# Second-weight sums on two engines, and preparation ahead of feed-forward items, in a fused attention and feed-forward kernel

## The chip, the cores and the metric

One core of a Trainium2 chip runs the whole program. The metric is the device time of one execution in microseconds (us); a comparison uses the median of several runs. The engines are TensorE (PE in the profile; PEld is its loading of weights), VectorE (DVE), ScalarE (ACT) and GpSimd (POOL); SyncE (SP) issues the transfers. Each engine works through its own queue in the order in which the program emitted its instructions, and waits on semaphores for the others.

## The reference

Two blocks follow each other. The first is routed attention over 4 batches, 8 heads, 768 positions and 64 values a head: every query and key is assigned to one of 16 clusters, and a query attends only to keys of its own cluster.

```python
q_assign = argmax(einsum('bhsd,hcd->bhsc', q_n, c_n))      # and k_assign
mask = q_assign[:, :, :, None] == k_assign[:, :, None, :]
attn = softmax(where(mask, scale * q @ k.T, -1e9))
x = (attn @ v) laid out as (3072 tokens, 512)
```

The second is a feed-forward block with 2048 hidden values: `h = x @ w_in`, `g = h * clip(h + 3, 0, 6) / 6`, `out = g @ w_out`. The weights arrive as 64-bit floats and are turned into 32-bit ones on the chip ("decoding").

## The kernel before

**Attention.** Two heads form a pair; there are 16 pairs of 12 steps each, 192 steps in all, and 48 steps make a batch. The main loop takes two steps at a time (n is the first of them, r its place in its pair). A step's scores are made by `scores` (PE, tile ps), turned into exponentials by `exponentials` (ACT, tile ex, line 463), and added up over keys by `key_sums` (POOL, tile acc, lines 484 and 487). `attn_v` multiplies ex with the values (PE, tile pv) and copies the result (ACT, num). After six steps `sum_up` adds acc over partitions (PE, tile pd, line 521), and `inverse` takes the reciprocal of pd on DVE (rcp, line 527) and multiplies num with it; a transfer keeps num in memory.

**Preparation of the next pair.** While a pair runs, the next one is prepared: `turn` transposes q and k on PE (pqk, line 318), ACT copies them (xf, line 324); `cluster_scores` makes pcs (line 335), copied by ACT to cs; `route` transposes it (pr), and DVE finds the maximum and the one-hot rows (lines 349, 355); `route_turn` transposes those (po, line 379), and ACT copies them to xm (line 384). Before step 96 (DECODED) the tiles pqk, pcs, pr, po, pd and the feed-forward's ph all take turns on two PSUM buffers (pool psum_m, tag m). From step 96 on, pqk, pcs, pr, po and pd share one PSUM buffer (pool psum_t), so that a pcs behind a pd waits for the reciprocal of that pd.

**Feed-forward.** A block is 256 tokens; the 12 blocks are worked off as "items" that the main loop takes from a list, fill, as steps allow. The first block's eight `up` items (PE, tile ph, line 643, then `lift` on ACT, `clip` on DVE and `gated_sums` on POOL, line 678) run singly at steps 60, 64, 70, 74, 80, 84, 90 and 94, and its seven `down` items (X and Y, line 723) after step 96. Products are in a form with seven multiplications instead of eight for each 2x2 split, so sums of weights are needed: `weight_sums` makes T1 to T4 of the second weights (line 577, two halves each, eight instructions on DVE; T3 overwrites a part of w_out_sb), and `make_first_sums` makes those of the first weights (line 610, four DVE instructions of 128x256 for each of eight i, called in the first block's down items: two in item 0, one in each later item). Down item 0 and 1 read T2, item 2 T1, item 3 T3, item 6 T4.

**The order.** It is written by hand: instructions are emitted in the order of the loop and no scheduler moves them. Within one pass of the loop before step 96: scores, exponentials, key sums, attn_v, the division if six steps are complete; then feed-forward items and preparation, one of each in turn, item first; then a number of decoding steps given by `share`. The list of decoding steps ends with the eight weight sums; share gives 6, 5, 4, 3, 5, 5 of them at r = 0, 2, 4, 6, 8, 10. So weight sums 0 to 2 fall at step 90 and 3 to 7 at step 92, and the division of step 92 (pd, rcp) stands among them on DVE.

Of the kernel before, what the change touches and what calls it, by code (L numbers as in the profile page):

```python
# [12 lines left out]
ALU = mybir.AluOpType  # L13
# [103 lines left out]
def fast_path(ctx, tc, ok, q, k, v, centroids, moe_w_in, moe_w_out, out):  # L117
# [3 lines left out]
    nc = tc.nc  # L121
    PSUM = bass.MemoryType.PSUM

    def pool(name, bufs, **kw):
        return ctx.enter_context(tc.tile_pool(name=name, bufs=bufs, **kw))
# [44 lines left out]
    st = {}  # L170
# [11 lines left out]
    def load(g, *names):  # L182
        if g >= NPAIR:
            return
        b, h = divmod(2 * g, H)
        for name in names:
            if name == "v":
                dst = st["v", g] = vp.tile([P, 2, NCH, D], F32, name="vt")
            elif name == "q":
                st["qk", g] = qkp.tile([P, 2, NCH, 2, D], F32, name="qk")  # L190
            if name != "v":
                dst = st["qk", g][:, "qk".index(name)]
            src = {"q": q, "k": k, "v": v}[name]
            for t in range(2):
                nc.sync.dma_start((dst[:, t] if name == "v" else dst[:, :, t]), src[b, h + t].rearrange("(p j) d -> p j d", p=P))
# [9 lines left out]
    def load_weights(i):  # L205
        if i < len(chunks):
            st["raw", i] = rawp.tile([P, WC, 2], U32, name="raw")
            nc.sync.dma_start(st["raw", i], chunks[i][1])
# [56 lines left out]
    def constants():  # L265
        make_identity(nc, ident)
        for t in range(2):
            nc.vector.tensor_reduce(
                out=parity[:, t : t + 1],
                in_=ident.rearrange("p (h t c) -> p t h c", t=2, c=C)[:, t], axis=AX.XY, op=ALU.max,  # L270
            )
        nc.gpsimd.memset(half_c, 0.5)
        nc.gpsimd.memset(low_c, 1.0 / BOUND)
        nc.gpsimd.memset(ones, 1.0)
        nc.gpsimd.memset(w_low, W_LOW)
        nc.gpsimd.memset(one_hot, 0.0)
        for c in range(C):
            nc.gpsimd.memset(number[:, 0, c : c + 1], c - C * (C - 1) / 2.0)
            nc.gpsimd.memset(number[:, 1, c : c + 1], -float(c))

        st["warm"] = psum_t.tile([P, 4, P], F32, name="warm", tag="t")
        idle(14)
# [5 lines left out]
    def centroid_norm():  # L288
        cn = unit_rows(nc, startp, cen, D)

        nc.scalar.activation(out=w_totals[:, 0, 0:1], in_=w_low, func=ACT.Exp)

        wide = startp.tile([P, 2, D], F32, name="cenwide")
        for t in range(2):
            nc.vector.tensor_scalar_mul(out=wide[:, t], in0=cn, scalar1=parity[:, t : t + 1])
        st["wide"] = wide
# [10 lines left out]
    def turn(g, part):  # L307
        if part == 0:
            st["xf", g] = xp.tile([P, NC2, P], F32, name="xf")
        qk, xf = st["qk", g], st["xf", g]  # L310
        pt = scratch([P, 4, P], "pqk")
        for i in range(4):
            j = part * 4 + i
            if g == 0 and j == NCH:

                idle(5)
                centroid_turn()
            nc.tensor.transpose(out=pt[:, i], in_=qk[:, j // NCH, j % NCH], identity=ident)  # L318
        dst = xf[:, part * 4 : part * 4 + 4]

        if g == 0 and part == 2:
            nc.vector.tensor_copy(out=dst, in_=pt)
        else:
            nc.scalar.copy(out=dst, in_=pt)
        if part == 2:
            st.pop(("qk", g))
# [4 lines left out]
    def cluster_scores(g):  # L331
        c0, xf = (2 * g) % H * C, st["xf", g]
        ps = scratch([P, 512], "pcs")[:, 0 : NC2 // 4 * P]
        for a in range(4):
            nc.tensor.matmul(  # L335
                ps[a * 2 * C : (a + 1) * 2 * C], lhsT=cnT[:, c0 : c0 + 2 * C], rhs=xf[:, a::4],
                start=True, stop=True,
            )
        cs = st["cs", g] = rtp.tile([P, NC2 // 4, P], F32, name="cs")
        nc.scalar.copy(out=cs, in_=ps)  # L340
# [168 lines left out]
    def divide(n):  # L509
        return sum_up(n)()  # L510
# [52 lines left out]
    wb = [[w_out_sb[:, t * HF : (t + 1) * HF, c * HC : (c + 1) * HC] for c in range(2)] for t in range(2)]  # L563

    def weight_sums(i):
        if i == 0:
            decoding.close()
            wtp = pool("wtp", 1)
            for name in ("T1", "T2", "T4"):
                st[name] = wtp.tile([P, HF, HC], F32, name=name)  # L570
            st["T3"] = wb[0][1]
        name, a, b = (
            ("T1", wb[0][1], wb[0][0]), ("T2", wb[1][1], st["T1"]), ("T4", wb[1][0], st.get("T2")),
            ("T3", wb[1][1], wb[0][1]),
        )[i // 2]
        h = slice(i % 2 * HF // 2, (i % 2 + 1) * HF // 2)
        nc.vector.tensor_tensor(out=st[name][:, h], in0=a[:, h], in1=b[:, h], op=ALU.subtract)  # L577

# [256 lines left out]
    per_pair = 2 * NCH  # L837
# [11 lines left out]
    READY, DECODED = per_batch + 2 * lag_d, 2 * per_batch  # L849

    def share(n, r):

        if n < READY:
            return {0: 4, 2: 3, 4: 3, 6: 1, 8: 2, 10: 4}[r]
        return {0: 6, 2: 5, 4: 4, 6: 3, 8: 5, 10: 5}[r]

    def items_by(n):

# [60 lines left out]
    with tc.manual_schedule():  # L919
        nc.scalar.dma_start(cen, centroids.rearrange("h c d -> (h c) d"))  # L920
        load(0, "q", "k")
        constants()
        load(0, "v")
        load_weights(0)
        centroid_norm()
        for part in range(3):
            turn(0, part)
        nc.vector.tensor_copy(out=ident_q, in_=ident)
        load(1, "q", "k")
        load_weights(1)  # L930
        cluster_scores(0)
        scores_qk(0)
        route(0)
        scores_qk(1)
        for part in range(2):
            route_turn(0, part)

        for n in range(0, total + lag_d + 2, 2):
            g, r = divmod(n, per_pair)
            fours = n >= DECODED  # L940
            steps = [i for i in (n, n + 1) if i < total]
            prep = prep_items(g + 1, r, fours)
            if fours:
                four_by_four(n, r, steps)
            else:
                for i in steps:
                    scores(i)
                    exponentials(i)
                    key_sums(i)
                for i in (n - lag_v, n - lag_v + 1):  # L950
                    if i >= 0:
                        attn_v(i)
                m = n - lag_d + 1
                if m >= 0 and m % NCH == NCH - 1:
                    later.append(divide(m))
                    ready(m)
            if prep and r == (6 if fours else 4):
                prep.pop(0)()
            if n == DECODED:
                st["early"] = False  # L960
            if r == 6 and not fours:
                load(g + 2, "q", "k")
                load(g + 1, "v")
            if not fours or r % 4 == 2 or n >= total:
                want = min(items_by(n + 2) - st["done"], len(fill))
                st["done"] += want
                for i in range(max(len(prep), want)):
                    if i < want:
                        fill.pop(0)()
                    if i < len(prep):  # L970
                        prep[i]()


                    for _ in range({6: 2 * (i > 0), 10: 2 * (i > 0)}.get(r, 2)):
                        if singles:
                            singles.pop(0)()
                if fours:
                    for op in singles + numbers:
                        op()
                    singles.clear(), numbers.clear()  # L980
            if r == 6 and fours:
                load(g + 2, "q", "k")
                load(g + 1, "v")
            for step in decode[: share(n, r)]:
                step()
            del decode[: share(n, r)]
            if not fours:
                for op in numbers:
                    op()
                numbers.clear()  # L990
                check_all()
            checks.extend(later)
            later.clear()

        while checks:
            check_all()
            checks.extend(later)
            later.clear()
        st["last"] = True
        flag = whether_good()  # L1000
        while fill:
            fill.pop(0)()
            if len(fill) == HOLD // 2:
                flag()
# [363 lines left out]
```

## Time and profile before

| what | value |
|---|---|
| median of 3 runs | 1006.48 us (1006.28 to 1008.38) |
| span of the profiled execution | 1007.6 us |
| PE busy | 987.3 us, 98% |
| DVE busy | 659.3 us, 65% |
| ACT, POOL busy | 389.5 us (39%), 431.7 us (43%) |
| PE idle in 125 to 150, 150 to 200, 200 to 225, 225 to 250 us | 2.05, 1.63, 2.02, 1.90 us |
| weight sums (line 577) | eight, 232.0 to 248.9 us, 1.22 us each at the shortest, 2.83 at the longest |
| steps 60 to 94 (first ph to last ph) | 138.0 to 240.9 us |

A row of a timeline gives the start, the duration, the engine, the line and operation, what is written from what, the shape, the count of equal instructions that follow each other, and in square brackets how long the engine had been idle and what it then waited for. A row with a count has the duration of all of them together. Windows give a stretch, its width, the busy time of each engine in it with the number of instructions, the granted clock of PE, the share of the transfer engines and GB/s.

### The profile page before, as it was taken

How to read it: one execution, taken by the hardware profiler on the slowest of the kernel's cores; microseconds unless marked ns; L12 is line 12 of the kernel's file. 1: busy time of each engine (PE TensorE's matmuls, PEld its weight loads, DVE VectorE, ACT ScalarE, POOL GpSimd, SP SyncE). 2: the span in 40 equal slices, each digit the busy share in tenths (PEclk: the TensorE clock that was granted, in tenths of full speed). 3: DMA queues.
4: the chain of work that ended last, by engine and by line, in shares of the span. 5: the costliest groups of instructions: out<-in, count | busy, mean ns of one | idle time of the engine just before them, and what ended most of it. 6: DMA issues, size and time to landing. Idle time of an engine off the chain costs nothing.

```text
span 1007.6 us, 16709 instructions
## 1 busy us (share of the span) xinstructions
PE 987.3 (98%) x6421; PEld 731.7 (73%) x6421; DVE 659.3 (65%) x1255; ACT 389.5 (39%) x762; POOL 431.7 (43%) x379
## 2 busy tenths in 40 slices
PE   8999999999999999999999999999999999999997
PEld 5444445545788777778787777777777898999996
DVE  6789988989856158376667577558657372727270
ACT  5888877684234134233333333333223020202020
POOL 3877766765425335335425335426336030303030
PEclk9999999999999999999999999999999999999999
DMA  7345554531253043123323224123123141414120
GB/s 188 94 126 147 143 171 131 154 83 53 98 165 100 14 128 92 39 69 104 85 83 95 56 82 109 37 71 101 36 79 92 34 142 36 132 40 129 48 69 25
DMA packets 91018, 92.70 MB, mean 92 GB/s; under 512 B 54321, under 2 KB 74801, under 8 KB 90929
## 3 DMA queue, kind: packets, MB, share of 16 engines
q1 hardware_dynamic: 90208, 90.98, 31.8%
q8 instruction: 53, 0.87, 0.4%
q10 hardware_dynamic: 720, 0.56, 0.2%
q14 instruction: 37, 0.29, 0.1%
HBM read 75.79 MB, written 15.73 MB: 91 GB/s over the span
## 4 chain that ended last, share of the span: by engine, by line
PE 73%; DVE 5%; ACT 1%; issue 1%; ACTq 0%; DVEq 0%
PE Y L723 17%; PE uY L688 14%; PE X L723 12%; PE uX L688 11%; PE ps L436 8%; PE pv L497 7%; PE pqk L318 1%; PE pd L521 1%; DVE sx L699 1%; PE ph L643 1%; DVE g_sb L699 1%; PE pcs L335 1%; DVE g_sb L556 1%; DVE ps L472 1%; DVE T L577 1%
## 5 line engine op out<-in xcount | busy, mean ns | idle before, releaser
L487 POOL TENSOR_TENSOR acc<-acc,ex 128x768 f32<-128x768 f32 x128 | 243.5, 1902 | 161.7 <-ACT ex L463 155.9
L678 POOL TENSOR_TENSOR g_sb<-g_sb 128x256 f32<-128x256 f32 x176 | 126.3, 739 | 281.3 <-DVE g_sb L556 269.7
L463 ACT ACTIVATE ex<-ps 128x768 f32<-128x768 f32 x192 | 147.4, 805 | 83.2 <-PE ps L436 64.0
L553 ACT ACTIVATE sx<-g_sb,half_c 128x512 f32<-128x512 f32 x88 | 63.5, 722 | 264.9 <-DVE g_sb L699 254.2
L436 PE MATMUL ps<-xf 64*128 64x384 f32 x768 | 157.0, 499 | 1.3 <-ACT ex L463 0.6
L497 PE MATMUL pv<-ex,vt 128*64 128x384 f32 x768 | 142.4, 499 | 0.4 <-ACT num L503 0.4
L497 PEld LDWEIGHTS pv<-ex,vt 128*64 128x64 f32 x768 | 48.4, 137 | 85.1 <-issue 74.9
L484 POOL TENSOR_TENSOR acc<-ex 128x768 f32<-128x768 f32 x32 | 59.1, 1846 | 103.3 <-ACT ex L463 103.2
L730 DVE TENSOR_TENSOR y<-y,Y 128x256 f32<-128x256 f32 x48 | 20.2, 421 | 125.5 <-PE Y L723 124.7
L472 DVE TENSOR_SCALAR ps<-xm,kid 128x384 f32<-128x384 bf16 x144 | 83.7, 616 | 26.4 <-ACT ex L463 23.2
L527 DVE RECIPROCAL rcp<-pd 128x384 f32<-128x384 f32 x32 | 81.7, 2554 | 24.4 <-PE pd L521 23.7
L436 PEld LDWEIGHTS ps<-xf 64*128 64x128 f32 x768 | 66.6, 188 | 40.6 <-issue 22.3
L688 PE MATMUL uX<-xb,w_in_sb 128*128 128x128 f32 x704 | 93.0, 275 | 0.0
L723 PE MATMUL X<-w_out_sb,g_sb 128*128 128x256 f32 x384 | 89.8, 382 | 0.0
L723 PE MATMUL Y<-T,g_sb 128*128 128x256 f32 x384 | 87.3, 380 | 0.0
L723 PE MATMUL Y<-w_out_sb,g_sb 128*128 128x256 f32 x384 | 87.1, 380 | 0.0
L688 PEld LDWEIGHTS uX<-xb,w_in_sb 128*128 128x128 f32 x704 | 85.7, 192 | 0.0
L723 PEld LDWEIGHTS X<-w_out_sb,g_sb 128*128 128x128 f32 x384 | 71.2, 190 | 13.1 <-issue 4.0
L723 PEld LDWEIGHTS Y<-T,g_sb 128*128 128x128 f32 x384 | 72.3, 190 | 11.2 <-issue 1.7
L723 PEld LDWEIGHTS Y<-w_out_sb,g_sb 128*128 128x128 f32 x384 | 72.3, 190 | 10.6 <-issue 1.1
L699 DVE TENSOR_TENSOR g_sb<-uY,sx 128x128 f32<-128x128 f32 (+1 forms) x176 | 65.7, 415 | 0.1
L556 DVE SCALAR_TENSOR_TENSOR g_sb<-sx,g_sb 128x512 f32<-128x512 f32 x88 | 64.4, 735 | 1.6 <-ACT sx L553 1.6
(120 smaller groups left out, 1437.6 us busy)
## 6 DMA issues: line engine op xcount, KB each, us to landing
tx<-td SPq DMA_DIRECT2D x86, 384.0 KB, 3.3
raw<-in_moe_w_in_dram SPq DMA_DIRECT2D x16, 512.0 KB, 4.3
raw<-in_moe_w_out_dram SPq DMA_DIRECT2D x16, 512.0 KB, 3.7
qk<-in_q_dram SPq DMA_DIRECT2D x32, 192.0 KB, 4.5
qk<-in_k_dram SPq DMA_DIRECT2D x32, 192.0 KB, 4.7
vt<-in_v_dram SPq DMA_DIRECT2D x32, 192.0 KB, 3.8
xd<-num SPq DMA_DIRECT2D x32, 192.0 KB, 2.4
xb<-xd SPq DMA_DIRECT2D x12, 512.0 KB, 4.2
```

The lines of the kernel that those rows point to most:

```text
L436: nc.tensor.matmul(st["ps", n][:, t, 0:HALF], lhsT=x[r, NCH + j], rhs=x[r, hf * NHC : (hf + 1) * NHC], start=first, stop=last, skip_group_ ...
L463: nc.scalar.activation(out=ex, in_=sc, func=ACT.Exp, scale=SM_SCALE)
L472: nc.vector.tensor_scalar(out=st["ps", n][:, t, 0:HALF].rearrange("p (a b) -> p a b", b=P), in0=st["xm", g][:, t * NCH + hf * NHC : t * NC ...
L487: nc.gpsimd.tensor_tensor(out=acc, in0=acc, in1=ex, op=ALU.add)
L497: nc.tensor.matmul(pv[t * D : (t + 1) * D], lhsT=vt[:, t, j], rhs=ex[:, t], start=(j == 0), stop=(j == NCH - 1),)
L527: nc.vector.reciprocal(out=rcp, in_=pd)
L553: nc.scalar.activation(out=r, in_=h, func=ACT.Relu, bias=half_c, scale=1.0 / 6.0)
L556: nc.vector.scalar_tensor_tensor(out=g, in0=r, scalar=1.0, in1=h, op0=ALU.min, op1=ALU.mult)
L678: eng.tensor_tensor(out=out_, in0=in0, in1=in1, op=op)
L688: nc.tensor.matmul(dst, lhsT=w[:, kt], rhs=x(kt), start=(kt == 0), stop=(kt == HK - 1))
L699: nc.vector.tensor_tensor(out=out_, in0=in0, in1=in1, op=ALU.add)
L723: nc.tensor.matmul(bank[:, half * HC : (half + 1) * HC], lhsT=g_sb[:, kind, i], rhs=w[:, i], start=(first and i == 0), stop=(last and i == ...
```

## The change

Three edits. The third and fourth weight sums change places in the list and go to GpSimd, while the first four halves (T1, T2) stay on VectorE. Their place in time moves: for the last pair before step 96, share gives fewer at r = 4 to 8, so that sum 0 falls at step 90 (behind the routing), 1 and 2 at step 92 (behind the division), and 3 to 7 at step 94. And before step 96 all preparation of a pass is emitted ahead of its feed-forward items, not in turn with them. The aim is to have the reciprocal and the one-hot rows less far back on VectorE, and the next pair ready earlier. What is computed stays as it was.

```diff
         name, a, b = (
-            ("T1", wb[0][1], wb[0][0]), ("T2", wb[1][1], st["T1"]), ("T4", wb[1][0], st.get("T2")),
-            ("T3", wb[1][1], wb[0][1]),
+            ("T1", wb[0][1], wb[0][0]), ("T2", wb[1][1], st["T1"]), ("T3", wb[1][1], wb[0][1]),
+            ("T4", wb[1][0], st.get("T2")),
         )[i // 2]
         h = slice(i % 2 * HF // 2, (i % 2 + 1) * HF // 2)
-        nc.vector.tensor_tensor(out=st[name][:, h], in0=a[:, h], in1=b[:, h], op=ALU.subtract)
+        eng = nc.vector if i < 4 else nc.gpsimd
+        eng.tensor_tensor(out=st[name][:, h], in0=a[:, h], in1=b[:, h], op=ALU.subtract)
...
         if n < READY:
             return {0: 4, 2: 3, 4: 3, 6: 1, 8: 2, 10: 4}[r]
-        return {0: 6, 2: 5, 4: 4, 6: 3, 8: 5, 10: 5}[r]
+        if n < DECODED - per_pair:
+            return {0: 6, 2: 5, 4: 4, 6: 3, 8: 5, 10: 5}[r]
+        return {0: 6, 2: 6, 4: 3, 6: 1, 8: 2, 10: 5}[r]
...
                 st["done"] += want
+                if n < DECODED:
+                    for make in prep:
+                        make()
+                    prep = []
                 for i in range(max(len(prep), want)):
```

## The prediction

> **What bounds the kernel now.** I read the busy shares first, then time slices of the stretch that the diff touches, then the queues of TensorE (PE), VectorE (DVE) and GpSimd (POOL) in order of time.
>
> ```profile
> PE 987.3 (98%) x6421; PEld 731.7 (73%) x6421; DVE 659.3 (65%) x1255; ACT 389.5 (39%) x762; POOL 431.7 (43%) x379
> ...
> 240.00:245.00 5.00, 3.10 (x21) 1.79 (x21) 4.97 (x5) 2.38 (x5) 1.88 (x1) 0.94 0.48 143
> 245.00:250.00 5.00, 5.00 (x24) 1.58 (x20) 4.97 (x7) 2.92 (x6) 0.36 (x1) 0.71 0.02 6
> ```
>
> PE is busy 98% of the span, so only time that PE loses can be won, and any new PE idle is lost whole. The second and third lines are slices (width, then PE, PEld, DVE, ACT, POOL busy, then granted clock): PE misses 1.90 us in 240 to 245, and the clock is 0.71 in 245 to 250.
>
> ```profile
> 237.18 3.72 PE L643 MATMUL ph<-xb,w_in_sb 128*128 128x256 f32 x16
> 242.74 0.50 PE L379 MATMUL po<-ident_q,one_hot 128*128 128x128 bf16 x6 [1.84 <-DVE rcp L527]
> ...
> 232.00 5.47 DVE L577 TENSOR_TENSOR T<-w_out_sb 128x1024 f32<-128x1024 f32 x2
> 237.40 2.83 DVE L577 TENSOR_TENSOR T<-w_out_sb,T 128x1024 f32<-128x1024 f32 x1
> 240.15 2.54 DVE L527 RECIPROCAL rcp<-pd 128x384 f32<-128x384 f32 x1
> 243.20 3.49 DVE L577 TENSOR_TENSOR T<-w_out_sb,T 128x1024 f32<-128x1024 f32 x3
> 246.61 2.35 DVE L577 TENSOR_TENSOR w_out_sb<-w_out_sb 128x1024 f32<-128x1024 f32 x2
> ```
>
> The cause: three weight sums (T1 twice, half of T2) stand ahead of the reciprocal on DVE. The reciprocal frees the PSUM buffer of pd, which the one-hot turn po takes next, so PE stands still for 1.84 us; then the clock halves. With it, the scores at 243.17 to the next ones at 248.30 take 5.13 us, where the same instructions at full clock sum to 0.97 + 1.07 + 1.44 = 3.48: 1.65 us lost.
>
> ```profile
> 249.63 3.45 POOL L678 TENSOR_TENSOR g_sb<-g_sb 128x256 f32<-128x256 f32 x4 [7.75 <-DVE g_sb L556]
> 253.04 1.99 POOL L484 TENSOR_TENSOR acc<-ex 128x768 f32<-128x768 f32 x1
> 255.11 3.83 POOL L487 TENSOR_TENSOR acc<-acc,ex 128x768 f32<-128x768 f32 x2
> 267.39 3.71 POOL L487 TENSOR_TENSOR acc<-acc,ex 128x768 f32<-128x768 f32 x2 [8.45 <-ACT ex L463]
> ...
> 253.40 3.87 DVE L610 TENSOR_TENSOR tx<-w_in_sb,tx 128x256 f32<-128x256 f32 x2
> 257.19 2.03 DVE L610 TENSOR_TENSOR w_in_sb<-w_in_sb 128x256 f32<-128x256 f32 x1
> 259.15 0.41 DVE L610 TENSOR_TENSOR tx<-w_in_sb 128x256 f32<-128x256 f32 x1
> 265.46 0.88 DVE L730 TENSOR_TENSOR y<-y,Y 128x256 f32<-128x256 f32 x2 [1.14 <-PE Y L723]
> 267.98 2.56 DVE L527 RECIPROCAL rcp<-pd 128x384 f32<-128x384 f32 x1 [1.65 <-PE pd L521]
> ...
> 272.17 0.85 PE L335 MATMUL pcs<-xf,cnT 128*32 128x384 f32 x8
> ```
>
> These lines carry the forecast. DVE's first-weight sums (L610) take 0.42 us each while POOL is idle (259.15) and about 1.95 us while POOL runs its 1.9 us key sums: one DVE sum per POOL instruction. The same shows on T: 1.22 us alone, 2.75 beside key sums. POOL is idle for 7.75 us before 249.63 and 8.45 us before 267.39, and in these two holes DVE gets through its T sums and L610 sums. The next reciprocal ends at 270.54, and pcs, which needs its PSUM buffer, starts at 272.17: slack 1.7 us.
>
> [...] half clock for some 3.4 us from 244.5, behind the 1.84 us gap, while gaps of up to 0.82 us drew none.
>
> **Part 1, preparation ahead of feed-forward items (batch 1, before step 96).** Eight such items run here. The code's order, followed through the two PSUM buffers of tag m, gives each its wait.
> - Step 60: eight pqk transposes (1.03 us, as at 175.00) now start at 138.03. ph then takes the first one's buffer, which ACT must copy out; ACT is in exponentials and the num copy until 139.87, the copy takes 0.58. ph starts at 140.50, lasts 3.56, scores at 144.06 instead of 143.60: +0.46. The old 0.82 gap goes, a 1.44 one comes.
> - Step 64 keeps its order: 0. Step 70: xm is copied under ph, the 0.30 wait goes: -0.30.
> - Step 74: ph waits for the copy of the last pqk, behind two exponentials that end at 181.5: 1.5 us of gap for the old 0.74 one: +0.6.
> - Step 80: ph waits 0.86 for the xm copy, against 0.40; later ACT waits shift too: +0.3.
> - Step 84: as step 60, +0.45.
> Sum by step 86: +1.5 us on PE. Lift and clip come later in each slot, so DVE idles ahead of them and its decoding backlog ends 3.4 us later (233.2 instead of 229.76).
> - Steps 90 to 94: pr and po stand ahead of ph. max and one-hot end at 234.4, just as PE reaches pd (234.4): 0. One T1 half (to 236.3) stands ahead of the reciprocal, which ends at 238.8. PE needs it for ph at 239.2: no gap. This saves the 1.84 us gap and the 1.65 us of half clock.
> Net of part 1 with the T split: X starts at 247.6 instead of 250.0, **2.4 us ahead**: +1.5 - 1.84 - 1.65, and 0.4 less because ph now hides the copy of xm that the scores at 244.1 waited for.
>
> **Part 2, T3 and T4 on GpSimd.** DVE loses four sums of 1.22 us: -4.87 us of its time, all of it in the POOL hole before 249.63. POOL gains four of 128x1024. No row has this; its two-input rows are 0.72 us for 256 and 1.81 for 768 elements, which gives 2.35 for 1024, my estimate. [...] DVE's own 1.22 would be the floor. I take 2.35, some 2.5 with a DVE sum between. POOL's order then is: four gated sums, T3, T3, T4, T4, three key sums. Clip ends at 244.5, so POOL runs without a hole to 244.5 + 4 x 0.87 + 4 x 2.5 + 3 x 1.95 = 263.9, and the key sums of steps 100 and 101 follow near 264.9.
> T3's and T4's readers don't wait: T3 is done at 253.6 and read at 259.6, T4 at 258.6 and read near 278.
> What waits is DVE. Behind T2 it has 20 L610 sums, one y0 add, two y1 adds and the reciprocal that pcs waits for. From 245.7 to 263.9 it gets one sum per POOL instruction: about 11. Nine remain: 9 x 0.44, adds 1.3, reciprocal 2.56, and 1.5 for each of two more key sums: 263.9 + 4.0 + 1.3 + 2.6 + 3.0 = 274.8, or 276 if a third key sum falls among them. PE reaches pcs at 272.2 - 2.4 = 269.8 and waits more than 5 us. Behind pcs in PE's queue stand X, Y and the next uX, so all of it moves. pcs starts near 275.6: **+3.4 us** against 272.17. [...] estimate 1.7 us, half of 3.4[...]. DVE's later sums (tx for uX) end at 281.4 and are read at 283.7, 2.3 us of slack, of which the later reciprocal uses the 1.6 that lay between its end (270.54) and pcs: no second wait. From there on PE is full to the end and nothing gives the time back.
> Sum: +3.4 + 1.7 = +5.1 us.
>
> **Rivals.**
> - A, as worked out, pcs waits for a late reciprocal: 1006.5 + 5.1 = 1011.6. Chance 0.48.
> - B, the goal is met: DVE gets in more than one sum per POOL instruction, or the hole before step 100 suffices, and pcs doesn't wait. For it: DVE does lose 4.87 us of work and its queue starts 3.7 us earlier (245.2 against 248.9). Against it: 253.4 to 259.2 shows one for one. 1006.5 - 2.4 = 1004.1. Chance 0.19.
> - C, half of it: the wait is 2 to 3 us and eats the gain: 1006.5, give or take 1.5. Chance 0.14.
> - D, A, and the new 1.4 to 1.5 us gaps at steps 60, 74 and 84 halve the clock as well (the old gap that did so was 1.84): two more at 1.7: 1015. Chance 0.19.
>
> **How the numbers follow.** A is likeliest: 1011.6. The range leaves out B and reaches from C's middle towards D: 1005.3 to 1015.4; POOL's price of 1.22 to 2.5 us moves A by up to 4.5 us down and is inside. Faster by 0.2% is below 1004.5: most of B and a little of C, 0.19. Within 0.2%: 0.14. Slower (above 1008.5): 0.67. The profiled span (1007.6) and the timed median (1006.5) differ by a us: a timed run may have lost less to the clock than the profiled one, which would only raise A.
>
> **What would show it.** A wait of PE at pcs (L335) for rcp of 4 to 6 us, L610 sums of 1.9 to 2.5 us between 246 and 264, POOL rows of T at about 2.4 us, no wait of po for rcp near 240, new waits of ph for ACT's xf of about 1.4 us, clock below 1 behind pcs. L610 near 0.45 us beside POOL's T sums would refute part 2; a pcs that doesn't wait would mean B.

## The result and the profile after

The changed kernel is slower. Its median is 1015.72 us (four runs, 1014.65 to 1018.33) against 1006.38 us for the kernel before on the same chip: ratio 1.0092, 95% interval 1.0067 to 1.0118. A second set (E11) gave 1015.4 against 1006.61: 1.0078, interval 1.0061 to 1.0095. The forecast was 1011.6 with a range up to 1015.4: the direction held, the size didn't, and the median lies 0.3 us above the range.

Line numbers of the changed kernel are higher by 2 behind line 570: L577 is L579, L610 is L612, L643 is L645. First the page's busy line, then two slices (width, then PE, PEld, DVE, ACT, POOL busy, then granted clock), of the changed kernel:

```profile
PE 988.9 (97%) x6421; PEld 732.8 (72%) x6421; DVE 663.1 (65%) x1251; ACT 388.8 (38%) x762; POOL 441.5 (43%) x383
...
275.00:280.00 5.00, 0.55 (x4) 0.20 (x8) 4.93 (x7) 0.00 (x0) 0.52 (x1) 0.70 0.28 105
280.00:285.00 5.00, 5.00 (x20) 3.45 (x13) 3.03 (x8) 1.69 (x5) 0.00 (x0) 0.62 0.31 118
```

PE's share fell from 98 to 97%. It is nearly idle in 275 to 280, and its clock is 0.70 of full speed in that slice and 0.62 in the next. PE's own row, in order of time, and what surrounds it on DVE and POOL (same kernel; the brackets give the idle time and what ended it):

```profile
142.50 3.72 PE L645 MATMUL ph<-xb,w_in_sb 128*128 128x256 f32 x16 [1.38 <-ACT xf L324]
154.90 3.72 PE L645 MATMUL ph<-xb,w_in_sb 128*128 128x256 f32 x16 [0.34 <-DVE rcp L527]
241.68 3.67 PE L645 MATMUL ph<-xb,w_in_sb 128*128 128x256 f32 x16
250.26 1.99 PE L725 MATMUL X<-w_out_sb,g_sb 128*128 128x256 f32 x8
267.31 0.87 PE L521 MATMUL pd<-acc,ones 128*64 128x384 f32 x4
279.45 1.51 PE L335 MATMUL pcs<-xf,cnT 128*32 128x384 f32 x8 [6.97 <-DVE rcp L527]
```

```profile
251.99 2.56 DVE L612 TENSOR_TENSOR tx<-w_in_sb 128x256 f32<-128x256 f32 x1
254.59 4.96 DVE L612 TENSOR_TENSOR tx<-w_in_sb,tx 128x256 f32<-128x256 f32 x2
264.03 3.86 DVE L612 TENSOR_TENSOR tx<-w_in_sb,tx 128x256 f32<-128x256 f32 x2
272.65 0.42 DVE L612 TENSOR_TENSOR w_in_sb<-w_in_sb 128x256 f32<-128x256 f32 x1
276.84 2.55 DVE L527 RECIPROCAL rcp<-pd 128x384 f32<-128x384 f32 x1
...
247.53 4.25 POOL L680 TENSOR_TENSOR g_sb<-g_sb 128x256 f32<-128x256 f32 x4 [2.89 <-DVE g_sb L556]
251.75 5.02 POOL L579 TENSOR_TENSOR w_out_sb<-w_out_sb 128x1024 f32<-128x1024 f32 x2
256.73 5.02 POOL L579 TENSOR_TENSOR T<-w_out_sb,T 128x1024 f32<-128x1024 f32 x2
261.71 2.00 POOL L484 TENSOR_TENSOR acc<-ex 128x768 f32<-128x768 f32 x1
263.79 7.75 POOL L487 TENSOR_TENSOR acc<-acc,ex 128x768 f32<-128x768 f32 x4
```

The wait of po near 240 is gone: po now runs at 241.33, and no bracket stands at the ph behind it (241.68). In its place pcs waits 6.97 us for the reciprocal. The reciprocal is late because POOL runs from 247.53 to 271.5 without a hole: 4 gated sums, 4 weight sums of 2.51 us, 5 key sums. Beside it a first-weight sum of DVE takes 2.56, 2.48 or 1.93 us, as long as POOL's instruction of that moment; at 272.65, with POOL idle, it takes 0.42. It isn't pd that is late: pd ran at 267.31, and the reciprocal begins at 276.84 with no idle time in front of it, so VectorE's own queue held it up. VectorE has four sums fewer than before (1251 instructions against 1255), and yet its busy time rose from 659.3 to 663.1 us.

This profile started 2.0 us late (scores at 136.11 instead of 134.11 before step 60, where no instruction had yet moved): some of its first matmuls were slow, the first pcs for example with 1.51 us instead of 0.85. The profile of before had an accident of its own, shown under E9. So the sums below compare E9 and E11, second profiles of the two kernels, whose starts differ by 0.20 us (scores at 132.54 and 132.74).

### The profile page after: what moved, and what is told of

Its sections match the earlier page's. It is cut to its first block, busy times and chain, and to the rows that moved or that the text cites. A ratio compares the mean times of both kernels' runs of the same rounds, so it can differ in the third digit from the quotient of the medians.

```text
span 1016.4 us, 16714 instructions
## 1 busy us (share of the span) xinstructions
PE 988.9 (97%) x6421; PEld 732.8 (72%) x6421; DVE 663.1 (65%) x1251; ACT 388.8 (38%) x762; POOL 441.5 (43%) x383
## 4 chain that ended last, share of the span: by engine, by line
PE 81%; DVE 11%; ACT 5%; issue 2%; DMA 1%; SPq 0%; ACTq 0%; DVEq 0%
PE Y L725 16%; PE uY L690 14%; PE X L725 11%; PE uX L690 11%; PE ps L436 11%; PE pv L497 9%; PE ph L645 2%; DVE tx L612 2%; ACT ex L463 2%; PE pqk L318 2%; PE pd L521 1%; DVE rcp L527 1%; PE pcs L335 1%; DVE wunit L247 1%; DVE sx L701 1%
```

## The experiments

Theory A: GpSimd's four sums close its hole (its idle stretch), VectorE's two-input sums go one for one beside GpSimd's instructions, the reciprocal comes late, pcs waits, and the clock halves behind the wait. Its rivals: R1, preparation ahead of items, with PE's waits for ACT's copies, is the cost. R2, POOL is merely late. R3, the loss is the clock's, drawn by the new small gaps. In every run but E9 and E10 T3 stands ahead of T4 in the list, as in the changed kernel. All times are medians, but for the single executions of E9 and E10; "before" is the median of the kernel before on the same chip. The ratio isn't the quotient of the two medians, which for E1 would be 1.0007.

| run | median us | before, us | ratio to before, 95% interval | wait of pcs, us |
|---|---|---|---|---|
| E1 all sums on VectorE | 1007.5 | 1006.76 | 0.9997 (0.9986 to 1.0007) | 0.60 |
| E2 no preparation ahead | 1012.95 | 1006.76 | 1.0054 (1.0037 to 1.007) | 6.52 |
| E3 only GpSimd | 1007.95 | 1006.76 | 1.0008 (1.0 to 1.0016) | none |
| E4 only preparation ahead | 1014.68 | 1006.76 | 1.007 (1.0053 to 1.0087) | none, but ph waits 5.05 |
| E5 only the share | 1004.87 | 1006.38 | 0.9983 (0.9974 to 0.9991) | none |
| E6 T4 alone on GpSimd | 1013.9 | 1006.38 | 1.0061 (1.0038 to 1.0084) | 4.03 |
| E7 preparation ahead at r = 10 only | 1005.05 | 1006.38 | 0.998 (0.9968 to 0.9991) | 0.61 |
| E8 fills in place of sums | 1005.98 | 1006.38 | 0.9989 (0.998 to 0.9999) | none |
| E11 the changed kernel again | 1015.4 | 1006.61 | 1.0078 (1.0061 to 1.0095) | 6.95 |

**E1, all sums on VectorE.** The changed kernel, but

```diff
-        eng = nc.vector if i < 4 else nc.gpsimd
+        eng = nc.vector
```

> The changed kernel with all eight weight sums on VectorE again; the share edit and the preparation edit stay. Theory A (the four sums on GpSimd close GpSimd's idle stretch before the key sums, VectorE's two-input sums then go one for one, the reciprocal comes late and pcs waits): the T3 and T4 sums run in GpSimd's hole or beside its gated sums, the reciprocal ends within 1.5 us of the time at which PE reaches pcs, no half clock follows pcs, and the median lies between 1004 and 1007.5 us, some 9 to 11 below the changed kernel. Rival R1 (the preparation edit costs most of it, by PE's waits for ScalarE's copies): no more than 3 us come back, 1012 to 1015. Rival R3 (the loss is the clock's, drawn by new gaps before step 96): also above 1011.

The loss goes: 1007.5, the upper edge of what A allowed, and the interval of the ratio includes 1. PE, DVE and POOL of this kernel:

```profile
269.95 0.85 PE L335 MATMUL pcs<-xf,cnT 128*32 128x384 f32 x8 [0.60 <-DVE rcp L527]
...
245.39 3.42 DVE L579 TENSOR_TENSOR w_out_sb<-w_out_sb 128x1024 f32<-128x1024 f32 x2
248.74 3.41 DVE L579 TENSOR_TENSOR T<-w_out_sb,T 128x1024 f32<-128x1024 f32 x2
...
264.51 3.82 POOL L487 TENSOR_TENSOR acc<-acc,ex 128x768 f32<-128x768 f32 x2 [6.79 <-ACT ex L463]
```

T3 and T4 cost DVE 6.8 us here, 1.7 each beside POOL's gated sums, and yet pcs waits only 0.60, because POOL keeps a hole of 6.79 us before step 100. The waits of ph for xf sum to 4.3 us in both kernels, and no slice of E1 behind them has a clock below 1.00, so R1 and R3 fall as the main cause.

**E2, no preparation ahead.** The changed kernel with preparation and items in turn.

```diff
-                if n < DECODED:
+                if n < 0:
                     for make in prep:
```

> The changed kernel with preparation and feed-forward items in turn again, as before; the weight sums stay on GpSimd and behind the division. Theory A: VectorE sets the start of pcs, so a PE that arrives earlier only waits longer: pcs waits 7.5 to 10 us for rcp instead of 6.97, the median is 1013 to 1016, within 3 us of the changed kernel. R1: the median falls by 5 us or more, to 1006 to 1010.

1012.95, just under A's range and above R1's; the wait stays:

```profile
273.67 1.51 PE L335 MATMUL pcs<-xf,cnT 128*32 128x384 f32 x8 [6.52 <-DVE rcp L527]
```

It is shorter than the 7.5 to 10 us that I expected: PE arrives earlier, but DVE's clip moves with PE (240.96 against 246.78, 2.1 us earlier once the starts, 132.38 and 136.11, are taken off), and the reciprocal ends 2 us earlier too.

**E3, only GpSimd.** The kernel before with T3 and T4 in the new order, on GpSimd, at the old place.

```diff
-        nc.vector.tensor_tensor(out=st[name][:, h], in0=a[:, h], in1=b[:, h], op=ALU.subtract)
+        eng = nc.vector if i < 4 else nc.gpsimd
+        eng.tensor_tensor(out=st[name][:, h], in0=a[:, h], in1=b[:, h], op=ALU.subtract)
```

> The kernel before with one edit: T3 and T4 on GpSimd (old share, old preparation), so that they run at step 92, one step pair earlier than in the changed kernel, and start in GpSimd's idle stretch of 7.75 us. Theory A: about three of the four GpSimd sums fit into that stretch, GpSimd's gated sums begin some 2 to 4 us late, VectorE gets its sums one for one over that much longer, and pcs waits 1 to 4 us; the wait of po for rcp (1.84 us before) stays. Median 1007.5 to 1012. R1: 1006.5, give or take 1. R2 (what counts is only that GpSimd's key sums come late and hold back the ex tiles): a wait of the scores' exponentials for ex, not of pcs for rcp.

1007.95, in A's range; but I was wrong on the wait: pcs doesn't wait. PE and POOL of this kernel:

```profile
243.57 0.50 PE L379 MATMUL po<-ident_q,one_hot 128*128 128x128 bf16 x6 [2.39 <-DVE rcp L527]
272.95 0.85 PE L335 MATMUL pcs<-xf,cnT 128*32 128x384 f32 x8
...
236.64 6.62 POOL L579 TENSOR_TENSOR w_out_sb<-w_out_sb 128x1024 f32<-128x1024 f32 x2
243.22 2.34 POOL L579 TENSOR_TENSOR T<-w_out_sb,T 128x1024 f32<-128x1024 f32 x1
247.19 2.36 POOL L579 TENSOR_TENSOR T<-w_out_sb,T 128x1024 f32<-128x1024 f32 x1 [1.63 <-DVE T L579]
...
268.18 3.70 POOL L487 TENSOR_TENSOR acc<-acc,ex 128x768 f32<-128x768 f32 x2 [5.40 <-ACT ex L463]
```

The four sums run from 236.64 to 249.55, while DVE is at T1, T2, the reciprocal and the division; two key sums are pushed behind them and fill POOL's first hole. The second hole, 5.40 us before 268.18, survives, and DVE works off its first-weight sums there. What grows is po's wait, from 1.84 to 2.39. So the four sums on GpSimd cost about 8 us at step 94 (the changed kernel against E1, and E2 against E5) and about 1 at step 92: the place decides.

**E4, only preparation ahead.** The kernel before with the third edit alone.

```diff
+                if n < DECODED:
+                    for make in prep:
+                        make()
+                    prep = []
```

> The kernel before with one edit: preparation ahead of feed-forward items before step 96; all sums on VectorE with the old share. Theory A: ph waits of 1.4 us at steps 60, 74, 84 and of 0.3 to 0.9 at 64 and 80, net +1.5 to +2.2 us on PE by step 86; the reciprocal of step 92 now stands behind the T sums still, but PE has ph to do before it needs the buffer. Median 1005.5 to 1009. R1: 1012 to 1015.

1014.68, far above the 1005.5 to 1009 of A and in the range of R1, but not for R1's reason: the waits for ACT's copies are 4.3 us as in E1. PE and DVE of this kernel show what is new:

```profile
243.80 6.33 PE L645 MATMUL ph<-xb,w_in_sb 128*128 128x256 f32 x16 [5.05 <-DVE rcp L527]
...
233.03 5.50 DVE L579 TENSOR_TENSOR T<-w_out_sb 128x1024 f32<-128x1024 f32 x2
238.46 2.82 DVE L579 TENSOR_TENSOR T<-w_out_sb,T 128x1024 f32<-128x1024 f32 x1
241.20 2.54 DVE L527 RECIPROCAL rcp<-pd 128x384 f32<-128x384 f32 x1
```

With the old share three T sums stand ahead of the reciprocal, and with po emitted ahead, the ph that used to run meanwhile comes behind it and wants the buffer of pd. The wait of 1.84 grows to 5.05, and 6.33 for that ph instead of 3.7 is half clock (the slices 240 to 245 and 245 to 250 have 0.73 and 0.59). My expectation, that PE "has ph to do before it needs the buffer", had the order wrong: it is that ph which needs it. So this edit needs the share edit; with it, it costs some 2.5 us (E5 to E1).

**E5, only the share.** The kernel before with the second edit alone.

```diff
-        return {0: 6, 2: 5, 4: 4, 6: 3, 8: 5, 10: 5}[r]
+        if n < DECODED - per_pair:
+            return {0: 6, 2: 5, 4: 4, 6: 3, 8: 5, 10: 5}[r]
+        return {0: 6, 2: 6, 4: 3, 6: 1, 8: 2, 10: 5}[r]
```

> The kernel before with one edit: the new share alone, so that the sums stand behind the routing and the division; all sums on VectorE, preparation and items in turn. Theory A': the share edit is the one that saves the wait of po (1.84 us) and the half clock behind it (1.65 us), and without GpSimd's sums nothing takes it back: no wait of po near 240, pcs waits 0 to 1 us, median 1002.5 to 1005, 1.5 to 4 us below before. Rival: moving the sums behind the division pushes the first-weight sums into the key sums by itself, pcs waits 3 us or more and the median is 1007 or above.

1004.87, with E7 the fastest: no wait of po near 240, none of pcs, no half clock.

```profile
239.23 0.50 PE L379 MATMUL po<-ident_q,one_hot 128*128 128x128 bf16 x6
267.25 0.85 PE L335 MATMUL pcs<-xf,cnT 128*32 128x384 f32 x8
```

This edit does what the change was for; the other two take it back.

**E6, half the dose.** The changed kernel with T3 on VectorE.

```diff
-        eng = nc.vector if i < 4 else nc.gpsimd
+        eng = nc.vector if i < 6 else nc.gpsimd
```

> Half the dose: the changed kernel, with T4 on GpSimd and T3 back on VectorE. Theory A (each GpSimd sum holds VectorE to one sum): GpSimd's chain ends about 5 us sooner, VectorE has two sums more; pcs waits 2.5 to 4.5 us instead of 6.97, half clock once, about 1.7 us or less; median 1010 to 1012.5, about midway between the changed kernel and the one with all sums on VectorE. Rival R4 (a threshold: any sum on GpSimd at that place delays the key sums past the next step): the wait stays at 6 us or more, 1014 to 1016.

```profile
276.13 1.36 PE L335 MATMUL pcs<-xf,cnT 128*32 128x384 f32 x8 [4.03 <-DVE rcp L527]
```

The wait grows with the dose, 0.60, 4.03 and 6.97 us for none, two and four sums on GpSimd, which speaks for A and against a threshold (R4). The median, 1013.9 (six runs, 1011.81 to 1015.53), lies above my 1010 to 1012.5 and its interval reaches that of the changed kernel: on the time alone this run is inconclusive. The profile says more. Its first matmuls took some 3 us longer than those of E9 and E11 (scores before step 60 at 135.75); from those scores to the end E6 takes 877.55 us, against 872.06 in the kernel before (E9), 872.71 in E1 and 880.86 in the changed kernel (E11). That lies between the two, as A has it.

**E7, a version meant to beat both.** E1's sums, with preparation ahead only at r = 10.

```diff
-                if n < DECODED:
+                if n < DECODED and r == 10:
```

> A version meant to beat both: all sums on VectorE, the new share, and preparation ahead of the item only where r is 10 (steps 70 and 94), where it hides the copy of xm; at steps 60, 64, 74, 80, 84 and 90 in turn as before. Theory A': no ph wait at 60, 74, 80, 84, no po wait, pcs waits under 1 us; 1002 to 1004.5. If the preparation at step 94 matters for VectorE's backlog, pcs waits 1 to 2 us and it is 1004.5 to 1006.

1005.05: above my 1002 to 1004.5, faster than both kernels, but not told apart from E5 by these times. The waits of 0.30 us for xm at steps 70 and 94 go, but pcs waits 0.61 again.

**E8, fills in place of sums.** T3 and T4 are left out; POOL fills the tiles with zero instead, which writes SBUF and reads nothing.

```diff
-        eng.tensor_tensor(out=st[name][:, h], in0=a[:, h], in1=b[:, h], op=ALU.subtract)
+        if i < 4:
+            eng.tensor_tensor(out=st[name][:, h], in0=a[:, h], in1=b[:, h], op=ALU.subtract)
+        else:
+            for _ in range(2):
+                eng.memset(st[name][:, h], 0.0)
```

> The changed kernel with each of the four GpSimd sums replaced by two fills with zero of the same 128x1024 (T3 and T4 are left out): GpSimd is held up for about as long but reads no SBUF. Theory A[...]: VectorE's first-weight sums beside the fills take 0.42 to 0.5 us, they are nearly done when GpSimd's key sums begin, pcs waits 0 to 2 us, median 1006 to 1009. Rival R2 (GpSimd's queue is merely late, and so the key sums lie where VectorE has its sums): the wait of pcs stays above 4 us, median above 1011. If the fills take much less than 2.3 us a pair, the comparison is weaker, and the rows of VectorE beside them decide.

1005.98, no wait of pcs. In this kernel L612 is L616; PE, POOL and DVE:

```profile
269.01 0.85 PE L335 MATMUL pcs<-xf,cnT 128*32 128x384 f32 x8
...
248.35 3.86 POOL L583 MEMSET w_out_sb<- 128x1024 f32 x4
252.15 3.86 POOL L583 MEMSET T<- 128x1024 f32 x4
...
249.06 0.89 DVE L616 TENSOR_TENSOR tx<-w_in_sb,tx 128x256 f32<-128x256 f32 x2
249.86 0.42 DVE L616 TENSOR_TENSOR w_in_sb<-w_in_sb 128x256 f32<-128x256 f32 x1
```

POOL is held up for 7.6 us (the sums took 10.0), and its key sums start only behind the fills, at 255.98. Counted from the scores before step 60, that is 5.3 us later than in E1, where the changed kernel (E11) is 7.6 later. DVE's sums beside the fills take 0.42 to 0.45 us instead of 2.5. So this much lateness alone doesn't do it, against R2. That VectorE's sums would take no longer beside fills than with GpSimd idle was an assumption of mine; these rows show it (0.42 to 0.45 us beside 0.42). In the changed kernel a two-input sum takes about as long as the GpSimd sum beside it (2.56 us beside 2.51); why a sum slows VectorE and a fill doesn't is not shown. The fills are 2.4 us shorter in all than the sums; the durations beside them, not the median, decide.

**E9, E10, E11, both kernels again, unchanged.** The device time is 1.8 us above the span (1006.42 and 1004.6 in E9), so the first profile of before, with a span of 1007.6, belonged to an execution of 1009.46 us, 3 above the median.

> The kernel before, unchanged, profiled again. Theory H (the half clock behind the 1.84 us wait of po is a matter of chance[...]): in an execution with a mean clock of 0.998 or 0.999 the wait of po is still about 1.84 us, but the clock stays at 1.00 in 240 to 250 and the matmuls between the scores take 1.65 us less; its span is near 1004.6. In one with 0.997 it looks like the first profile (1007.6). If a 0.999 execution shows the half clock too, the baseline does not explain the size of the miss.

> The kernel before, unchanged, a third profile, for the same question: with the half clock a span of 1006 to 1007.6, without it 1004 to 1005; the wait of po is 1.84 us in both.

> The changed kernel, unchanged, for a second profile and more times: the wait of pcs for rcp is 6.9 to 7.1 us again (it is set by the order of the queues, not by chance), half clock for 3.4 to 6.8 us behind it; the start-up before step 60 may differ by up to 2 us from the first profile. Median 1014 to 1016.

PE of the kernel before, in E9 and behind the second dots in E10:

```profile
241.17 0.50 PE L379 MATMUL po<-ident_q,one_hot 128*128 128x128 bf16 x6 [1.84 <-DVE rcp L527]
242.90 0.81 PE L436 MATMUL ps<-xf 64*128 64x384 f32 x4
243.64 1.51 PE L497 MATMUL pv<-ex,vt 128*64 128x384 f32 x8
...
268.95 0.85 PE L335 MATMUL pcs<-xf,cnT 128*32 128x384 f32 x8
280.52 0.61 PE L688 MATMUL uX<-xs,tx 128*128 128x128 f32 x4
...
241.40 0.50 PE L379 MATMUL po<-ident_q,one_hot 128*128 128x128 bf16 x6 [1.83 <-DVE rcp L527]
243.87 1.51 PE L497 MATMUL pv<-ex,vt 128*64 128x384 f32 x8
```

The wait is there, 1.84 us, but the scores and pv behind it take 0.81 and 1.51, where the first profile had 1.49 and 2.46 at half clock. E10 is the same (wait 1.83, span 1004.7). First profile and E9 differ by 3.0 us of span: 1.57 of start, up to the scores before step 60, and 1.65 behind po make 3.2, a little more than all of it. The half clock behind this wait comes and goes between executions of one kernel. How often is not shown. Of 59 executions of the kernel before, run beside E5 to E8, 43 took 1005.88 to 1006.90 us at a mean clock of 0.998 or 0.999, and 16 took 1007.95 or more, 13 of them at 0.997, the clock of the first profile (E9 and E10 have 0.998). That many of the 16 had the half clock is an inference; a late start adds as much. E11 repeats the changed kernel; below PE's rows its slices:

```profile
276.08 1.51 PE L335 MATMUL pcs<-xf,cnT 128*32 128x384 f32 x8 [6.95 <-DVE rcp L527]
290.16 0.61 PE L690 MATMUL uX<-xs,tx 128*128 128x128 f32 x4
...
270.00:275.00 5.00, 0.00 (x0) 0.00 (x0) 4.90 (x7) 0.05 (x1) 2.03 (x1) 0.95 0.48 184
275.00:280.00 5.00, 3.92 (x14) 2.24 (x15) 4.62 (x10) 1.69 (x5) 0.00 (x0) 0.50 0.11 39
280.00:285.00 5.00, 5.00 (x24) 4.27 (x23) 1.51 (x4) 0.37 (x1) 0.00 (x0) 0.87 0.28 105
```

The wait is the same within 0.02 us in both profiles, as a wait set by the order of the queues would be.

## Why the prediction was right on the way and short on the size

Right: the wait of po is gone; ph waits for xf are 1.38, 1.53 and 1.38 us where 1.4 to 1.5 was forecast; POOL's T sums take 2.51 (2.5 with a DVE sum between); DVE's sums beside POOL take 1.93 to 2.57 (1.9 to 2.5); pcs waits for rcp and half clock follows. Rival D fell: behind the gaps of 1.4 to 1.5 us the clock stayed at 1.00. B and C fell with the wait.

Short: the sum. Measured here is E11 against E9, with 0.20 us of start taken off:

| term | forecast | measured |
|---|---|---|
| half clock behind po, saved | -1.65 | 0 |
| rest of part 1, PE's arrival at pcs (+1.5 - 1.84 - 0.4) | -0.75 | -0.02 (269.13 - 0.20 - 268.95) |
| wait of pcs (275.6 - 269.8) | +5.8 | +6.95 |
| half clock behind it | +1.7 | +2.5 (pcs to uX 14.08, against 11.57) |
| given back later | 0 | -0.6 |
| sum | +5.1 | +8.8 (1013.6 - 1004.6 - 0.2) |

- **"1.65 us lost", and "This saves the 1.84 us gap and the 1.65 us of half clock".** The largest term. I took a loss of the one profiled execution as a saving and subtracted it from a median whose executions, by their times and by E9 and E10, mostly didn't have it. The prediction saw the sign of it ("a timed run may have lost less to the clock than the profiled one, which would only raise A") and then didn't raise A. Worked on the median, A is 1006.5 + 5.1 + 1.65 = 1013.2.
- **"Step 64 keeps its order: 0", and "Sum by step 86: +1.5 us on PE".** Step 64 didn't keep it: ph waits 0.34 us there for rcp. With that, and with the other items a little larger than forecast, part 1 cost 2.22 us by step 86 (215.14 - 0.20 - 212.72). Behind it PE won back 2.24, the 1.84 and the 0.4 of the forecast, so that nothing is left of the 0.75.
- **"nine remain ... 274.8, or 276 if a third key sum falls among them".** A third key sum did, and POOL had no hole near 264. On the forecast's time (E11 plus 1.37 us, the difference of the starts) clip ended at 245.5 instead of 244.5, and the gated sums took 4.25 us instead of 3.48: half of T2 ran beside them (in E6, with three such halves beside them, they took 5.85). So the reciprocal came 1.8 us later than forecast and PE only 0.7, which makes the wait 6.95 instead of 5.8.
- **"estimate 1.7 us, half of 3.4".** That half clock would follow the longer wait was my estimate, from the one wait of 1.84 us, and I counted on one stretch of it. The slices of E11 miss 0.25, 2.5 and 0.65 us of clock, 3.4 in all: two such stretches. The first began inside the wait, and what fell behind the wait's end cost the path 2.5 us (2.1 in the first profile, pcs to uX 13.67).
- "From there on PE is full to the end and nothing gives the time back": 0.6 us do come back (the shift is 9.63 up to 422 us, 9.38 behind 445 and 9.0 at the end, start included). They lie at no wait that the profile names, and their cause stays open.

The edits can be added up in the profiles, from the scores before step 60 to the end: the kernel before takes 872.06 us (E9), with the share 870.19 (E5), with preparation ahead as well 872.71 (E1), with the sums on GpSimd as well 880.86 (E11). That is -1.9, +2.5 and +8.2, together +8.8; the medians, which come from different chips, give -1.5, +2.6 and +8.2. The order of adding matters: alone, preparation costs 8 (E4) and the sums on GpSimd 1.2 (E3).

## What to carry to other kernels

Moving work off a busy engine can slow that engine down (VectorE's sums took 0.42 us with GpSimd idle, 1.93 to 2.56 beside its key and weight sums): before handing a two-input sum to GpSimd, look for the idle stretch of GpSimd in which VectorE has been catching up, and don't fill that one; the stretch at step 92, in which VectorE was busy with other things, cost about 1 us to fill instead of 8. An edit that brings work ahead of an item must be followed to the next user of the same buffer, since the item itself may be what covered a wait. And a gain counted from a profile is checked against the times: where the profiled execution lies above the median, part of its loss may be chance, which no change can win.

## What the runs showed of the hardware

- A wait of 1.84 us of PE drew half clock (0.50 granted from 245 to 247 us) in one of three profiled executions, which I had taken from that one profile as a certainty. A wait of 2.39 us (E3, 0.67 in 245 to 250) drew it in its one profile, waits of 4.03 us and more (E2, E4, E6, the changed kernel, lowest slice 0.50 to 0.66) in every one, and waits up to 1.54 us, between 20 and 310 us, in none: away from the longer waits every slice has 1.00.
- The clock that the slices miss is about 1.7 us behind the waits of 1.84, 2.39 and 4.03 us, and 3.4 us behind those of 5.05 to 6.97 us: 3.4 or 6.8 us at half clock, and nothing between, in seven profiles.
- A 128x256 sum of VectorE took 0.42 us with GpSimd idle, 1.93 beside key sums of 1.94 and 2.48 to 2.56 beside weight sums of 2.51: each time about as long as GpSimd's instruction.
- A 128x1024 fill on GpSimd took 0.95 us, a sum of that size 2.34 to 2.54 and, beside VectorE's own sums of that size (E3), 3.33; VectorE's sums beside the fills took as little as with GpSimd idle.
